# Four chunks' transposes moved from TensorE to the DMA crossbar, with the stores moved to ScalarE's queue

## The chip, the cores and the metric

One core of a Trainium2 chip. The metric is the device time of one execution in microseconds (us), median of several; runs of one kernel are compared with runs of the kernel before on the same chip in the same rounds. Besides the time, each execution gives the mean clock granted to TensorE (1.0 is full speed), and it is fast or slow (slow is over 1.5% above the fastest run of the same kernel). The experiments ran on several chips, so each is compared by its ratio to the kernel before on its own chip.

## The reference

A linear recurrence per head (retention), then a gated feed-forward layer on its output:

```python
def _attn_ref(q, k, v):                  # (4, 8, 768, 64) each
    gamma = 1.0 - 2.0 ** (-5.0 - np.arange(H))
    for t in range(S):
        state = gamma[None, :, None, None] * state + np.einsum('bhd,bhe->bhde', k[:, :, t], v[:, :, t])
        y[:, :, t] = scale * np.einsum('bhd,bhde->bhe', q[:, :, t], state)
# x = y as 3072 tokens of 512
def _moe_ref(x, w_gate, w_val, w_out):   # 512 -> 1536 -> 512
    gate = 1.0 / (1.0 + np.exp(-(x @ w_gate)))
    return gate * (x @ w_val) @ w_out
```

## The kernel before

The recurrence is computed in 24 chunks of 128 tokens. Per chunk k and q are loaded as bf16 (by GpSimd's queue, which casts), v as float32; k and q must be transposed for the scores. Chunks 0 to 11 are transposed on TensorE through PSUM (the memory that TensorE writes), with a copy back by ScalarE; chunks 12 to 23 by the DMA crossbar, that is by a DMA that transposes while it moves the data. Six blocks of 512 tokens (`t`) run the feed-forward groups, and the attention steps of the next block are put between those groups at the indices in `place`.

```python
XBAR = 12
def transposes(g):                       # chunks 4..11
    ...                                  # 8 TensorE transposes into PSUM tile tp
    nc.scalar.activation(qkT[g], tp, AX.Copy)

def xbar(g):                             # chunks 12..23
    qkT[g] = ld.tile([128, 2 * NP, C], BF16, tag="qkX", name="qkX", bufs=8)
    for i, x in enumerate((kn[g], qn[g])):
        nc.sync.dma_start_transpose(out=qkT[g][:, i * NP:(i + 1) * NP, :],
                                    in_=x.rearrange("s h d -> s (h d)"))

def down(t, sm, part):
    ...                                  # 12 matmuls into o
    ob = ffn.tile([128, D_MODEL], F32, tag="ob", name="ob")     # 3 buffers
    nc.scalar.copy(ob, o)
    nc.sync.dma_start(out=out[row:row + 128, :], in_=ob)
...
for t in range(NT):
    ...
    if t + 2 < NT:
        for g in range(4 * t + 8, 4 * t + 12):
            load_chunk(g)                # GpSimd's queue, in order
    for i, group in enumerate(groups):
        if i == len(groups) - 9:
            for g in range(4 * t + 8, 4 * t + 12):
                if XBAR <= g < NG:
                    xbar(g)
        group()
        ...                              # the attention steps whose place is i
```

Each engine takes its instructions in the program's order.

## Time and profile before

| | kernel before |
|---|---|
| time, median of the three runs at that point | 236.8 us |
| TensorE (PE) busy | 225.4 us of a span of 235.7, 1712 matmul records |
| ScalarE (ACT) busy | 91.0 us |
| DMA | full to about 124 us, then nearly idle |

The main lines of its page stand in the prediction below. First, what SyncE's own queue (SPq) waited for (who, for whom, us in total, times, longest), where the stores are L299:

```profile
SPq L299 <- ACT ob L297: 163.5, 22, 42.5
SPq L164 <- DMA kn<-in_k_dram: 15.4, 4, 9.4
```

The stores wait for the copies that fill their buffer, and SyncE can afford to wait. Second, ScalarE in time (start, duration, operation, in brackets the idle time before it and what ended it) in block 0:

```profile
47.89 0.59 ACT L297 COPY ob<-ff 128x512 f32<-128x512 f32 x1 [0.27 <-PE ff L292]
48.84 1.02 ACT L148 ACTIVATE qkT<-tp 128x1024 bf16<-128x1024 bf16 x1 [0.37 <-PE tp L146]
```

An output tile is copied, then, 0.4 us later, chunk 6's transposes are copied. On ScalarE there is no store between the two.

### The profile page before, as it was taken

How to read it: one execution, taken by the hardware profiler on the slowest of the kernel's cores; microseconds unless marked ns; L12 is line 12 of the kernel's file. 1: busy time of each engine (PE TensorE's matmuls, PEld its weight loads, DVE VectorE, ACT ScalarE, POOL GpSimd, SP SyncE). 2: the span in 40 equal slices, each digit the busy share in tenths (PEclk: the TensorE clock that was granted, in tenths of full speed). 3: DMA queues.
4: the chain of work that ended last, by engine and by line, in shares of the span. 5: the costliest groups of instructions: out<-in, count | busy, mean ns of one | idle time of the engine just before them, and what ended most of it. 6: DMA issues, size and time to landing. Idle time of an engine off the chain costs nothing.

```text
span 235.7 us, 4320 instructions
## 1 busy us (share of the span) xinstructions
PE 225.4 (96%) x1712; PEld 117.8 (50%) x1738; DVE 103.9 (44%) x178; ACT 91.0 (39%) x173; POOL 92.3 (39%) x111
## 2 busy tenths in 40 slices
PE   6779999999999999999999999999999999999994
PEld 5655644555555554444554444544444554444444
DVE  3465436375656741346641346641346641234301
ACT  8765334345455521334323333233333331333211
POOL 8999865687887367964111001111000000000000
PEclk9999999999999999999999999999999999999999
DMA  7999999999999999999992342012100012100022
GB/s 132 188 187 166 196 204 207 191 241 224 225 172 135 149 151 216 241 116 118 141 161 91 90 92 45 1 47 90 44 3 0 0 47 82 52 0 3 0 89 89
DMA packets 77555, 27.27 MB, mean 116 GB/s; under 512 B 65056, under 2 KB 73120, under 8 KB 77536
## 3 DMA queue, kind: packets, MB, share of 16 engines
q0 software_dynamic: 57616, 16.78, 69.3%
q1 hardware_dynamic: 19776, 10.16, 21.2%
q8 instruction: 13, 0.21, 0.4%
q10 hardware_dynamic: 144, 0.07, 0.1%
q14 instruction: 6, 0.05, 0.1%
HBM read 28.31 MB, written 6.29 MB: 147 GB/s over the span
## 4 chain that ended last, share of the span: by engine, by line
PE 87%; DMA 6%; POOL 3%; issue 1%; ACT 1%; DVE 1%; SPq 0%; ACTq 0%; POOLq 0%
PE ff L261 50%; PE ff L292 25%; DMA wv<-in_moe_w_val_dram 3%; PE sA L179 3%; DMA vf<-in_v_dram 3%; PE y L215 2%; PE y L191 2%; PE tp L146 2%; PE z L201 2%; PE ff L312 1%; POOL vs L169 1%; PE ff L275 1%; POOL wg L81 1%; ACT ob L297 1%; ACT qkT L148 0%
## 5 line engine op out<-in xcount | busy, mean ns | idle before, releaser
L266 DVE TENSOR_TENSOR hT<-gs,ff 128x512 bf16<-128x512 f32 (+1 forms) x72 | 48.8, 677 | 76.1 <-PE ff L261 74.5
L261 PE MATMUL ff<-xT,wg 128*128 128x512 bf16 (+1 forms) x276 | 71.5, 375 | 1.3 <-DVE xT L223 0.7
L261 PE MATMUL ff<-xT,wv 128*128 128x512 bf16 (+1 forms) x282 | 71.8, 375 | 0.9 <-DMA wv<-in_moe_w_val_dram 0.5
L265 ACT ACTIVATE gs<-ff 128x512 f32<-128x512 f32 (+1 forms) x72 | 42.3, 588 | 67.5 <-PE ff L261 67.0
L292 PE MATMUL ff<-wo,hT 128*128 128x512 bf16 x268 | 62.2, 379 | 0.6 <-issue 0.2
L261 PEld LDWEIGHTS <-wv 128*128 128x128 bf16 x288 | 28.1, 98 | 33.4 <-DMA wv<-in_moe_w_val_dram 0.9
L261 PEld LDWEIGHTS <-wg 128*128 128x128 bf16 x288 | 26.6, 98 | 30.4 <-issue 1.1
L292 PEld LDWEIGHTS <-hT 128*128 128x128 bf16 x276 | 26.0, 98 | 30.3
L297 ACT COPY ob<-ff 128x512 f32<-128x512 f32 x23 | 13.5, 586 | 50.6 <-PE ff L292 45.4
L169 POOL TENSOR_TENSOR vs<-vf,tabv 128x512 bf16<-128x512 f32 x14 | 14.5, 1047 | 46.6 <-PE y L215 41.3
L223 DVE TENSOR_TENSOR xT<-y,taby 128x512 bf16<-128x512 f32 x24 | 16.4, 685 | 20.9 <-PE y L215 20.9
L62 POOL DMA_DIRECT2D vf<-in_v_dram x23 | 20.7, 902 | 10.7 <-DMA kn<-in_k_dram 4.6
L67 POOL DMA_DIRECT2D kn<-in_k_dram x23 | 20.8, 903 | 6.2 <-DMA qn<-in_q_dram 2.2
L184 DVE TENSOR_TENSOR stA<-sA,causal 128x512 bf16<-128x512 f32 x24 | 16.5, 687 | 14.5 <-PE sB L179 14.4
L68 POOL DMA_DIRECT2D qn<-in_q_dram x23 | 20.4, 886 | 6.0 <-DMA vf<-in_v_dram 2.8
L209 ACT CAST zbd<-z 64x256 bf16<-64x256 f32 x40 | 14.7, 366 | 12.5 <-PE z L201 12.2
L185 DVE TENSOR_TENSOR stB<-sB,causal 128x512 bf16<-128x512 f32 x24 | 16.3, 681 | 0.0
L148 ACT ACTIVATE qkT<-tp 128x1024 bf16<-128x1024 bf16 x8 | 8.2, 1024 | 5.0 <-PE tp L146 5.0
L215 PE MATMUL y<-stB,vs 128*64 128x128 bf16 x96 | 9.5, 221 | 0.4 <-DVE stB L185 0.4
L215 PE MATMUL y<-stA,vs 128*64 128x128 bf16 x96 | 9.6, 221 | 0.0
L304 PE MATMUL ff<-ident 128*128 128x128 bf16 x82 | 7.1, 249 | 1.6 <-POOL ident masks.py:199 1.6
L169 DVE TENSOR_TENSOR vs<-vf,tabv 128x512 bf16<-128x512 f32 x10 | 6.9, 690 | 3.8 <-DMA vf<-in_v_dram 3.7
(58 smaller groups left out, 123.7 us busy)
## 6 DMA issues: line engine op xcount, KB each, us to landing
vf<-in_v_dram POOLq DMA_DIRECT2D x23, 256.0 KB, 8.4
out_dram<-ob SPq DMA_DIRECT2D x23, 256.0 KB, 2.0
kn<-in_k_dram POOLq DMA_DIRECT2D x23, 128.0 KB, 8.6
qn<-in_q_dram POOLq DMA_DIRECT2D x23, 128.0 KB, 8.7
wg<-in_moe_w_gate_dram POOLq DMA_DIRECT2D x6, 256.0 KB, 7.1
wv<-in_moe_w_val_dram POOLq DMA_DIRECT2D x6, 256.0 KB, 7.6
wo<-in_moe_w_out_dram POOLq DMA_DIRECT2D x4, 384.0 KB, 10.3
kf<-in_k_dram SPq DMA_DIRECT2D x1, 256.0 KB, 3.4
```

The source lines that it names most:

```text
L62: eng.dma_start(out=vf[g], in_=src(v, g))
L67: nc.gpsimd.dma_start(out=kn[g], in_=src(k, g))
L68: nc.gpsimd.dma_start(out=qn[g], in_=src(q, g))
L169: eng.tensor_tensor(vs[g], vf[g], tabv[:, g % NCH, :].unsqueeze(2).to_broadcast([C, H, D]), op=ALU.mult)
L184: nc.vector.tensor_tensor(stA[g], sc[g][0], causal4, op=ALU.mult)
L185: nc.vector.tensor_tensor(stB[g], sc[g][1], causal4, op=ALU.mult)
L215: nc.tensor.matmul(y[g][i * D:(i + 1) * D, p, :], vs[g][:, 2 * p + i, :], st[:, p, :], start=(first and p == 0), stop=True, skip_group_che ...
L223: nc.vector.tensor_tensor(xT[g // 4][:, :, col:col + C], y[g], taby[:, :, c * C:(c + 1) * C], op=ALU.mult)
L261: nc.tensor.matmul(u[:, lo:hi], w[:, kk, n1 * 128:(n1 + 1) * 128], xT[t][:, kk, lo:hi], start=(kk == 0), stop=(kk == KT - 1))
L265: nc.scalar.activation(gs[:, lo:hi], ps[0][:, lo:hi], AX.Sigmoid)
L266: nc.vector.tensor_tensor(hT[t][:, n1, lo:hi], gs[:, lo:hi], ps[1][:, lo:hi], op=ALU.mult)
L292: nc.tensor.matmul(o, hT[t][:, n1, sm * 128:(sm + 1) * 128], wo[:, n1, :], start=(n1 == 0), stop=(n1 == NFF - 1))
```

## The change

Its intent: TensorE loses 32 transposes and ScalarE four copies, as the crossbar transposes chunks 8 to 11 as soon as they land. So that nothing disturbs this, the loads of chunks 12 to 15 are held until chunk 11's k transpose is there, by a one-element GpSimd copy that reads it. SyncE's queue now waits for loads early on, so the stores go to ScalarE's queue.

```diff
-    XBAR = 12
+    XBAR = 8
+    mark = const.tile([1, 1], BF16, name="mark")
-        scale_v(g, nc.vector if g < XBAR else nc.gpsimd)
+        scale_v(g, nc.vector if g < 12 else nc.gpsimd)
-        nc.sync.dma_start(out=out[row:row + 128, :], in_=ob)
+        nc.scalar.dma_start(out=out[row:row + 128, :], in_=ob)
@@ block t == 1
-            place = [p + 2 for p in place]
+            place = [4, 5, 5, 8, 8, 11, 11, 14, 18]
+        if t == 1:
+            nc.gpsimd.tensor_copy(mark, qkT[11][0:1, 0, 0:1])
         if t + 2 < NT:
             for g in range(4 * t + 8, 4 * t + 12):
                 load_chunk(g)
+                if t == 0:
+                    xbar(g)
@@ the later blocks transpose as before
-                    if XBAR <= g < NG:
-                        xbar(g)
+            if t > 0 and i == len(groups) - 9:
+                ...                      # xbar of the next four chunks
```

## The prediction

> **What bounds the kernel now.** I read the head of the page first, then the chain of work that ended last, then the groups, the DMA issues, and last the time-ordered list around the instructions that the change touches. The page of the kernel before:
>
> ```profile
> PE 225.4 (96%) x1712; PEld 117.8 (50%) x1738; DVE 103.9 (44%) x178; ACT 91.0 (39%) x173; POOL 92.3 (39%) x111
> ...
> PE   6779999999999999999999999999999999999994
> ...
> DMA  7999999999999999999992342012100012100022
> ...
> PE 87%; DMA 6%; POOL 3%; issue 1%; ACT 1%; DVE 1%; SPq 0%; ACTq 0%; POOLq 0%
> ```
>
> The reader is to see that TensorE (PE) is full from the fourth slice on (a slice is 235.7 / 40 = 5.9 us), and that 87% of the chain is PE. Only the first 23 us belong to the loads, and the change leaves them alone. So the time falls only where PE has fewer instructions or a shorter wait. The second resource is the DMA: nines until about 21 x 5.9 = 124 us, then nearly idle. Each chunk's loads run in that full stretch, though PE rarely feels them, since they were issued early enough. The change spends this second resource to relieve the first.
>
> What can be relieved is small. From the groups, sorted by cost:
>
> ```profile
> L148 ACT ACTIVATE qkT<-tp 128x1024 bf16<-128x1024 bf16 x8 | 8.2, 1024 | 5.0 <-PE tp L146 5.0
> ...
> L146 PE MATMUL tp<-ident,qn 128*128 128x128 bf16 x32 | 3.1, 219 | 0.0
> L146 PE MATMUL tp<-ident,kn 128*128 128x128 bf16 x32 | 3.1, 219 | 0.0
> ```
>
> These are chunks 4 to 11, eight transposes each. The 219 ns is a latency; they are pipelined, and the chain merges one chunk's eight into a piece of 0.45 us (four such pieces for chunks 8 to 11: 0.46, 0.45, 0.45, 0.45). The busy column (3.1 + 3.1 for eight chunks) counts the last latency too, so I take the 0.45.
>
> **What the Trainium skill says.** "VectorE: DVE Perf Modes", section The three transpose paths, gives 390 ns for a 128x128 transpose on TensorE and 1309 ns through the DMA crossbar. In this trace the TensorE one costs about 0.45 / 8 = 0.056 us in a row: seven times less than the page's isolated figure, so the saving must not be taken from the page. "DMA: Bandwidth & Descriptors", section Issuing engines are not separate DMA queues, says that issuing from several engines saves only issue time, as all run on the same 16 DMA engines; so moving stores to ScalarE frees SyncE's queue but no bandwidth. The trace agrees that sharing hurts:
>
> ```profile
> 58.00:70.00 12.00, 11.66 (x112) 6.79 (x111) 7.10 (x12) 5.83 (x10) 9.77 (x12) 1.00 1.88 205
> 70.00:82.00 12.00, 11.89 (x105) 6.39 (x106) 8.29 (x14) 6.06 (x11) 6.71 (x9) 1.00 1.74 142
> ...
> 131.70:143.00 11.30, 11.25 (x82) 5.35 (x81) 6.09 (x10) 4.13 (x8) 0.38 (x1) 1.00 0.50 108
> ```
>
> In this table by stretch the last three columns are granted clock, DMA share and GB/s. The crossbar transposes of chunks 12 to 15 were issued from 66.8 to 82 us: total rate fell from 205 to 142 GB/s. Alone (131.7 to 143 us) a transpose landed in 2.4 to 4.0 us; among loads in 8.1 to 13.2 us. The same page, section Silent corruption: two transposing streams in flight at once, asks that transposes stay on one stream; all 24 before, and all 32 after, are SyncE's, so the stores may sit on ScalarE.
>
> **The change part by part.**
>
> Removed on PE: 32 transposes, 4 x 0.45 = 1.8 us, all on the path, as PE is full there.
>
> Removed on ScalarE: 4 copies of 1.02 us, beside PE but for one place. The time-ordered list shows it (start, duration, engine, operation; in brackets the idle time before it and what ended it):
>
> ```profile
> 60.07 0.39 PE L146 MATMUL tp<-ident,qn 128*128 128x128 bf16 x4
> ...
> 60.55 1.02 ACT L148 ACTIVATE qkT<-tp 128x1024 bf16<-128x1024 bf16 x1 [0.67 <-PE tp L146]
> ...
> 61.63 0.23 PE L179 MATMUL sA<-qkT 64*128 64x128 bf16 x1 [0.28 <-ACT qkT L148]
> ```
>
> Chunk 8's scores stood behind this copy, with PE idle for 0.3 us (its weight loads 0.45). I take 0.4 us gained.
>
> Added on ScalarE: 23 store issues. The one store that ScalarE issues in the kernel before took 0.37 us, so 23 x 0.37 = 8.5 us less 4 x 1.02 = 4.1 us: 4.4 us more on an engine at 39%. It counts only where ScalarE is on PE's path, and I find one place, late in the first token block:
>
> ```profile
> 52.44 0.59 ACT L297 COPY ob<-ff 128x512 f32<-128x512 f32 x1 [2.57 <-PE ff L292]
> ...
> 52.95 1.02 ACT L148 ACTIVATE qkT<-tp 128x1024 bf16<-128x1024 bf16 x1
> ...
> 54.07 0.23 PEld L179 LDWEIGHTS <-qkT 64*128 64x128 bf16 x8 [0.42 <-ACT qkT L148]
> ```
>
> The copy of an output tile is followed at once by chunk 7's copy, for which PE waits, and from there masks and xT lead to the next block's first matmul at 56.45. The store's issue now lies between the two copies: about 0.4 plus the wait for the copy to finish, so I charge 0.5 us. Later blocks have no such copy.
>
> Added on the DMA: 8 crossbar transposes while it is full. Loads of chunk 8 were issued at 45.94 and 46.92 and took 7.2 and 7.9 us, so k lands at 53.1 and q at 54.8. SyncE has no stores now, so it issues at once; with the 8.1 to 8.7 us of the first transposes under load, chunk 8's are there at 63.5. Who needs them: scores of chunk 8 moved from place 3 to place 5. Group 3 ended near 61.2 before, less the 0.45 of transposes, plus two groups of 1.73 us (8 matmuls of 0.216): 64.2, plus the 0.5 charged above: 64.7. Margin about 1 us. Chunk 9: q landed at 58.4, say 1.5 later now because of the transposes, plus 8.5: 68.5; scores at place 8 near 70.3. Chunk 10: 61.4 + 3 + 10 = 74.4 against 76.4. Chunk 11: about 77 against 82. The margins are thin but positive; I charge 0.4 us for one that fails.
>
> The hold: chunk 12's load was issued at 58.9 and now waits for chunk 11's transpose, 72 to 76. From there GpSimd issues 24 loads (0.9 us each, 21.6 at least; before, 58.9 to 91.0 = 32 us, of which some 8 were backlog that is now gone): 24 us, so the GpSimd multiplication for chunk 12, queued behind them, starts at 96 to 100 instead of 91.0. It is needed by chunk 12's state matmuls, at 106.3 before, 104.6 after. Chunk 12's own transposes should land near 92, against 97. So the hold is hidden, with 4 to 5 us to spare. The small GpSimd copy itself is nothing.
>
> Sum: 236.8 - 1.8 - 0.4 + 0.5 + 0.4 = **235.5 us**, 0.5% less.
>
> **The rivals.** First, the crossbar is late: chunks 8 to 10 each stall PE. For it: latencies of 10 to 13 us with several in flight, and margins of 1 to 2 us; against it: with loads 12 and on held back, less is in the queues than at 66 to 82 us. Three stalls of 1 us make 238. Second, the hold comes out too long, and chunk 12's scaled values or transposes are late: a stall near 97 to 105 us, 1 to 5 us, 236 to 240; against it are the 4 us worked out above and a DMA drained when the hold ends. Third, all is hidden and the ScalarE charge too (PE has other work queued): the full 2.2 us, 234.5. Fourth, ScalarE becomes the bound by its stores: 39% busy plus 2% speaks against it.
>
> **Range and chances.** The best case is 1.8 + 0.4 plus a little, 234.2; two late transposes or a small stall from the hold give 237.4. Faster by over 2% would need 4.7 us, twice what can be removed: 0.02. Slower by over 2% needs nearly 7 us of stalls over the gain: 0.03.
>
> **What would show it.** PE's instruction count falls by 32, its busy time by about 1.8 us (225.4 to 223.6); the group of qkT copies shrinks from 8 to 4. Waits of PE on DMA (qkX) at the scores of chunks 8, 9, 10 show the first rival; PE waiting on GpSimd's vs near 100 us, or on qkX near 97, the second. Chunk 7's scores starting 0.5 us later confirm the charge for the stores. The prediction is wrong if PE's idle time between 60 and 110 us grows by more than 2 us, or if the first 23 us differ.

## The result

| | before | changed |
|---|---|---|
| time, all runs (us) | 236.72 to 237.47 | 259.07, 259.28, 260.21, 265.02, 268.34 |
| median (of four runs each, without 259.07) | 236.95 | 262.62 |
| TensorE clock | 1.0 | 0.96 in the fast runs, 0.94 to 0.947 in the slow |
| TensorE busy (us), matmul records | 225.4, 1712 | 229.8, 1679 |

Fast runs against fast runs, the ratio is 1.0949 (95% interval 1.0909 to 1.0989): **9.5% slower**, far outside the predicted range. A ratio here is the mean time of one kernel's fast runs over that of the other's of the same rounds, so it is not quite the ratio of the medians; the changed kernel's fast runs are the three up to 260.21. The profile of the changed kernel is of a slow run (265.02 us, span 263.3); the runs differ in the clock, and the reading below is checked against experiments whose profiles are fast. Its page (in the two rows of 40 digits, a digit is the busy share of TensorE, and the clock granted to it, in tenths, in one of 40 equal slices):

```profile
PE 229.8 (87%) x1679; PEld 118.4 (45%) x1706; DVE 103.8 (39%) x178; ACT 87.5 (33%) x169; POOL 92.4 (35%) x112
...
PE   6979999600999999925999999999999999999994
...
PEclk9999999965599999985999999999999999999999
```

TensorE has two holes, in slices of 6.6 us: at 46 to 66 us and at 112 to 125 us. In and after each the granted clock drops (the slices' means go down to 0.5), so 33 fewer matmul records take 4.4 us longer. (The weight loads fell by the expected 32, from 1738 to 1706; some matmul records are missing from both traces.) The waits, in the columns used above:

```profile
ACT qkT L149 <- DMA qkX<-qn: 16.8, 1, 16.8
PE sA L180 <- ACT qkT L149: 15.5, 1, 15.5
...
PE ff L262 <- ACT ob L298: 8.0, 2, 7.6
ACT ob L298 <- DMA qkX<-kn: 8.0, 1, 8.0
ACT ob L298 <- DMA qkX<-qn: 5.9, 1, 5.9
```

TensorE waits for ScalarE, and ScalarE waits for crossbar transposes. The first of these is odd: `qkT L149` is chunk 6's copy out of PSUM, which has nothing to do with a DMA. ScalarE in time, at the place shown of the kernel before:

```profile
47.65 0.59 ACT L298 COPY ob<-ff 128x512 f32<-128x512 f32 x1 [0.27 <-PE ff L293]
64.61 0.34 ACTq L300 DMA_DIRECT2D out_dram<-ob  x1
64.99 1.02 ACT L149 ACTIVATE qkT<-tp 128x1024 bf16<-128x1024 bf16 x1 [16.76 <-DMA qkX<-qn]
```

The output tile was ready at 48.24, but its store was issued only at 64.61. Chunk 8's q transpose was issued at 55.35 and took 9.2 us: it landed at 64.5. So the **store** waited for that transpose, and chunk 6's copy stood behind the store. The chain of work that ended last has it in these words (start, duration, what), and the second hole below it:

```profile
55.35 9.18 DMA qkX<-qn
64.61 0.34 ACTq L300
...
109.64 10.68 DMA qkX<-kn
120.39 0.34 ACTq L300
```

Why would a store to memory wait for a transpose of other data? The built program says so. A semaphore is a counter that one engine or DMA raises and another waits for. In this program every hardware-queue DMA (those of SyncE and ScalarE) gets one of eight completion semaphores in turn, and before it reuses one, its engine must wait for the DMA that had it before. The start of that list, read from the built program and not from a profile, in the order in which the semaphores are handed out:

```
engine   DMA                  semaphore   must first have landed
SyncE    loads k0, q0, v0     0, 1, 2
SyncE    transpose k8, q8     3, 4
SyncE    transpose k9, q9     5, 6
SyncE    transpose k10, q10   7, 0        -, load k0
ScalarE  block 0 store 1      1           load q0 (long done)
SyncE    transpose k11, q11   2, 3        load v0, transpose k8
ScalarE  block 0 store 2      4           transpose q8
SyncE    transpose k12, q12   5, 6        transposes k9, q9
ScalarE  block 0 store 3      7           transpose k10
...
ScalarE  block 1 store 1      5           transpose k15
ScalarE  block 1 store 2      6           transpose q15
ScalarE  block 1 store 3      1           transpose k17
```

"DMA: Bandwidth & Descriptors" of the Trainium skill, section Why a DMA increments its semaphore by 16 and not by 1, gives a reason that fits such waits: two DMAs in flight on one semaphore can fool a waiter, so it asks for one per slot in flight. No run here shows a fooled waiter. Its section Anatomy of one DMA, which describes the path of GpSimd's DMAs, says where a wait is served: "any semaphore wait happens on the issuing sequencer before dispatch". The trace agrees with this for ScalarE's stores: store 2 was issued 0.1 us after q8 had landed, and block 1's third store was issued at 120.39, when k17 (issued at 109.64, 10.7 us) had just landed; that is the second hole.

The loss of this slow, profiled run adds up. Against the repaired kernel of the experiments (span 233.9, PE busy 223.8, as many matmul records): 15.5 us of waiting for chunk 6's copy, 8.0 for the output copies, and 229.8 - 223.8 = 6.0 us of slower clock make 29.5; the spans differ by 263.3 - 233.9 = 29.4 us. The fast runs (spans of 257.4 to 258.5) lose 23.5 to 24.6 us; how that splits no profile shows.

### The profile page after: what moved, and what is told of

Its sections match the earlier page's. It is cut to its first block, busy times and chain, and to the rows that moved or that the text cites. A ratio compares the mean times of both kernels' runs of the same rounds, so it can differ in the third digit from the quotient of the medians.

```text
span 263.3 us, 4259 instructions
## 1 busy us (share of the span) xinstructions
PE 229.8 (87%) x1679; PEld 118.4 (45%) x1706; DVE 103.8 (39%) x178; ACT 87.5 (33%) x169; POOL 92.4 (35%) x112
## 4 chain that ended last, share of the span: by engine, by line
PE 68%; DMA 19%; POOL 8%; issue 2%; ACT 1%; DVE 1%; SPq 0%; ACTq 0%; POOLq 0%
PE ff L262 39%; PE ff L293 20%; DMA wo<-in_moe_w_out_dram 4%; DMA qkX<-kn 4%; DMA wg<-in_moe_w_gate_dram 4%; DMA qkX<-qn 3%; DMA kn<-in_k_dram 3%; PE sA L180 2%; PE y L216 2%; POOL wg L81 1%; POOL wv L81 1%; POOL qn L68 1%; PE z L202 1%; PE y L192 1%; POOL vf L62 1%
## 5 line engine op out<-in xcount | busy, mean ns | idle before, releaser
L262 PE MATMUL ff<-xT,wg 128*128 128x512 bf16 (+1 forms) x276 | 72.7, 380 | 9.0 <-ACT ob L298 7.6
L262 PE MATMUL ff<-xT,wv 128*128 128x512 bf16 (+1 forms) x283 | 72.8, 378 | 0.8 <-ACT ob L298 0.5
L293 PE MATMUL ff<-wo,hT 128*128 128x512 bf16 x266 | 64.0, 387 | 0.7 <-issue 0.2
L180 PE MATMUL sA<-qkT 64*128 64x128 bf16 x32 | 3.4, 229 | 15.6 <-ACT qkT L149 15.5
L149 ACT ACTIVATE qkT<-tp 128x1024 bf16<-128x1024 bf16 x4 | 4.1, 1025 | 19.9 <-DMA qkX<-qn 16.8
L180 PEld LDWEIGHTS <-qkT 64*128 64x128 bf16 x64 | 2.0, 98 | 17.7 <-ACT qkT L149 16.6
## 6 DMA issues: line engine op xcount, KB each, us to landing
wo<-in_moe_w_out_dram POOLq DMA_DIRECT2D x4, 384.0 KB, 10.7
```

Source lines behind the costliest of these rows:

```text
L262: nc.tensor.matmul(u[:, lo:hi], w[:, kk, n1 * 128:(n1 + 1) * 128], xT[t][:, kk, lo:hi], start=(kk == 0), stop=(kk == KT - 1))
L293: nc.tensor.matmul(o, hT[t][:, n1, sm * 128:(sm + 1) * 128], wo[:, n1, :], start=(n1 == 0), stop=(n1 == NFF - 1))
```

## The experiments

**Theory** (rotation): stores on ScalarE wait for transposes that had their semaphore before them, and hold up ScalarE. **Rivals**: the crossbar or the hold is too slow in a full DMA; three output buffers are too few; or ScalarE's stores beside transposes are slow in themselves.

### 1. The stores back on SyncE

```diff
-        nc.scalar.dma_start(out=out[row:row + 128, :], in_=ob)
+        nc.sync.dma_start(out=out[row:row + 128, :], in_=ob)
```

> The change with one part undone: the stores go back to SyncE's queue. Theory (semaphore rotation: each hardware-queue DMA must wait until the DMA eight places earlier in the program's order has landed, and a store on ScalarE holds up ScalarE's copies while it waits): the wait of 16.8 us of chunk 6's copy vanishes, but the four stores of block 0 now stand on SyncE behind chunk 11's transposes, which wait for loads until about 70 us; with three output buffers the fourth output copy at about 56 us waits for the first store, to about 72 to 75 us, and ScalarE stalls there: 245 to 255 us. Rival (the crossbar itself is too slow or the hold too long, with stores irrelevant): stalls stay at the scores of chunks 8 and 12, about 258 us.

Measured: 253.75 us (ratio 1.0709, 1.0656 to 1.0762). Its waits:

```profile
ACT ob L298 <- DMA out_dram<-ob: 18.2, 1, 18.2
PE ff L262 <- ACT ob L298: 15.8, 1, 15.8
```

As the theory said: the wait of chunk 6's copy is gone, and the other one is there, the fourth output copy (run at 74.17 us) waiting for the first store, now behind the transposes on SyncE. So with the stores on SyncE three buffers are too few, which is a loss of its own.

### 2. The stores on SyncE and eight output buffers

```diff
+        nc.sync.dma_start(out=out[row:row + 128, :], in_=ob)
-    ob = ffn.tile([128, D_MODEL], F32, tag="ob", name="ob")
+    ob = ffn.tile([128, D_MODEL], F32, tag="ob", name="ob", bufs=8)
```

> Stores back on SyncE's queue and eight output buffers instead of three, so that nobody waits for a late store. Rotation theory: nearly all of the loss is gone, 234.5 to 236.5 us, as the prediction reckoned without its ScalarE charge; no wait of ScalarE on a DMA longer than 1 us. Rival (crossbar or hold): PE still waits for qkX or vs, over 245 us.

Measured: 235.51 us (ratio 0.9936, 0.9906 to 0.9966). That is 0.6% less than the kernel before. The whole loss is gone, with the crossbar, the hold and the places untouched. The page:

```profile
PE 223.8 (96%) x1679; PEld 116.4 (50%) x1706; DVE 104.3 (45%) x178; ACT 87.2 (37%) x169; POOL 92.2 (39%) x112
...
PE   6879999999999999999999999999999999999994
```

No hole is left, and PE's busy time is down from 225.4 to 223.8.

### 3. Eight buffers alone, and the stores on ScalarE with eight

The kernel before, and the changed kernel, each with `bufs=8` for `ob` and no other edit.

> The kernel before with eight output buffers and nothing else: the control for the runs with eight. Its stores hardly ever made ScalarE wait, so 236.5 to 237.3 us, no different from before. If it is faster by 1 us or more, the gain of the eight-buffer run is not the transposes'.

Measured: 236.49 us (0.9986, 0.997 to 1.0002): no different, so experiment 2 owes nothing to the buffers by themselves.

> The change with eight output buffers instead of three, stores on ScalarE. Its list of waits for stores is that of the change. Rotation theory: the buffers do not help, as it is the store itself that waits on ScalarE: 255 to 265 us, with the copy of chunk 6 again waiting some 16 us. Rival (the loss is that three output buffers are too few for late stores): about 236 us.

Measured: 252.99 us in its one fast run, 261.66 to 266.33 in three slow ones; no ratio could be given. Its profile (slow) has the same wait:

```profile
ACT qkT L149 <- DMA qkX<-qn: 17.0, 1, 17.0
```

Buffers do not remove the wait where the store itself blocks the engine. The rival that too few buffers explain the changed kernel's loss falls; whether they take off some of it (252.99 against 259.07 to 260.21, one run on another chip) stays open.

### 4. The kernel before with only the stores moved

```diff
-        nc.sync.dma_start(out=out[row:row + 128, :], in_=ob)
+        nc.scalar.dma_start(out=out[row:row + 128, :], in_=ob)
```

> The kernel before with only the stores moved to ScalarE's queue; no transpose added, no load held. Rotation theory, from the list of the program's waits: block 0's stores wait for nothing late, but block 1's first store shares its semaphore with chunk 16's k transpose, the second with its q, the third and fourth with chunk 17's; these land at about 94 to 103 us while the copies are ready at 86 to 95, so ScalarE stops in block 1: 243 to 252 us. Rival (the loss comes from the added transposes or the hold; my original charge for the move): 236.5 to 237.5 us.

Measured: 241.28 and 241.34 us in the fast runs, 246.01 and 250.44 in the slow (ratio of the fast 1.0178, 1.0133 to 1.0223, so by the 2% rule unclear, though clear of 1). Slower by 1.8% without a single added transpose, a little less than I expected (243 to 252 us). Its ScalarE in block 1:

```profile
85.63 0.59 ACT L297 COPY ob<-ff 128x512 f32<-128x512 f32 x1 [2.81 <-PE ff L292]
92.49 0.34 ACTq L299 DMA_DIRECT2D out_dram<-ob  x1
92.87 0.75 ACT L209 CAST zbd<-z 64x256 bf16<-64x256 f32 x2 [6.66 <-DMA qkX<-kn]
```

The copy was ready at 86.2, its store left at 92.49, and the state's copy stood behind it: block 1's first store shares its semaphore with k16, exactly as the list says. In block 0, where the list has no such pair, all four stores left at once. There, too, my original charge can be read: chunk 7's copy began 1.00 us after the output copy instead of 0.51, close to the 0.5 us charged.

### 5. One place more in the rotation

One load of 256 bytes on SyncE between chunk 9's and chunk 10's transposes of the changed kernel, which does nothing but take a semaphore:

```diff
                 if t == 0:
                     xbar(g)
+                    if g == 9:
+                        nc.sync.dma_start(out=junk, in_=v[0, 0, 0:1, :])
```

> The change with one tiny extra load of 256 bytes on SyncE's queue between chunk 9's and chunk 10's transposes; it does nothing but take one place in the rotation of the eight semaphores. By the list of the program's waits block 0's second store now waits for chunk 9's k transpose instead of chunk 8's q. Rotation theory: the long wait of chunk 6's copy on ScalarE ends when chunk 9's k has landed, at about 66 to 68 us, instead of 64.5 (chunk 8's q): 2 to 3 us longer. Rival (a fixed hardware order or a full DMA): it ends at 64.5 as before.

Measured: 258.73 us (one run, state unknown). ScalarE in time:

```profile
46.92 0.59 ACT L299 COPY ob<-ff 128x512 f32<-128x512 f32 x1 [0.27 <-PE ff L294]
68.30 0.34 ACTq L301 DMA_DIRECT2D out_dram<-ob  x1
68.69 1.02 ACT L150 ACTIVATE qkT<-tp 128x1024 bf16<-128x1024 bf16 x1 [21.17 <-DMA qkX<-kn]
```

In this run chunk 8's q landed at 54.74 + 8.1 = 62.8 us and chunk 9's k at 56.17 + 12.1 = 68.3 us. The store left at 68.30. One unrelated tiny DMA moved the wait from one transpose to the next, 5.5 us here (I had said 2 to 3, from the landings of the first profile). The total of one run says little, but the moment at which the store left is the plainest evidence of the rotation.

### 6. The stores on ScalarE, but the rotation in step

k and q of a chunk share one tile and one transpose, so that four transposes and four stores per block could fill the eight semaphores in step:

```diff
-        for i, x in enumerate((kn[g], qn[g])):
-            nc.sync.dma_start_transpose(out=qkT[g][:, i * NP:(i + 1) * NP, :],
-                                        in_=x.rearrange("s h d -> s (h d)"))
+        nc.sync.dma_start_transpose(out=qkT[g], in_=kq[g].rearrange("s h d -> s (h d)"))
@@ first attempt, block 1: the hold also waits for a hidden tile of the block
+                nc.gpsimd.tensor_copy(mark, hT[1][0:1, 0, 0:1])
@@ second attempt, instead of that: in xbar, before the transpose
+        if g >= 12 and g % 4 == 0:
+            nc.vector.memset(qkT[g][0:1, 0, 0:1], 0.0)
```

> The change as it is, stores on ScalarE, hold kept, but k and q of a chunk share one tile and are transposed by one DMA of 128x1024 instead of two of 128x512, and the marker copy on GpSimd also waits for the first hidden tile of block 1, which only moves chunk 12's transposes behind block 0's stores in the order in which semaphores are handed out. Same bytes, same engines, same queues. Rotation theory: no store of block 0 shares a semaphore with a transpose in flight, so the 16.8 us wait and nearly all the loss vanish: 234.5 to 238 us (block 1's last stores share with chunks 14 and 15, perhaps 1 or 2 us of wait). Rival (transposes beside loads, stores on ScalarE as such): 255 to 260 us as before.

Measured: 259.18 us median (fast run 250.27; the others and the profile slow). A miss in size: block 0's stores all left at once, but in block 1 the third and fourth stores waited 8.1 and 7.8 us for chunks 14 and 15, which the list does name and which I had put at 1 to 2 us. I had the pairs right and the landings wrong.

> The change with stores still on ScalarE and the hold kept; one transpose DMA of 128x1024 per chunk, and a one-element VectorE memset into the first target tile of each later block (12, 16, 20) just before its transposes, so that in the order in which the eight semaphores are handed out four transposes and four stores alternate. By the list of the program's waits no store now waits for a transpose that could be in flight (the one shared with chunk 11's is long done). Rotation theory: ScalarE's waits on qkX are gone in blocks 0 and 1, where the run before it still had 8.1 and 7.8 us of them in block 1 as its list says (chunks 14 and 15): 236 to 240 us, the rest being chunk 8's scores waiting about 3 us for the longer single transpose. Rival (stores on ScalarE beside transposes are slow in themselves, or the DMA is too full): 250 us or more.

Measured: 242.87, 244.61 and 245.78 us fast (ratio 1.0318, 1.026 to 1.0376). No store waits for a transpose any more; the waits left:

```profile
ACT ob L299 <- DMA out_dram<-ob: 5.9, 2, 3.9
PE z L203 <- POOL vs L171: 3.2, 1, 3.2
PE sA L181 <- DMA qkX<-kq: 2.1, 1, 2.1
```

So issuing stores on ScalarE beside transposes does not cost the 250 us or more of the rival. But the time is above my 236 to 240: the single transpose is late for chunk 8 (2.1 us), with three buffers two copies wait for earlier stores to land (3.9 us at most), and GpSimd's multiplication for chunk 12 comes 3.2 us late (below).

### 7. Without the hold

Experiment 2 without the GpSimd copy that holds the loads of chunks 12 to 15.

> Stores on SyncE, eight output buffers, and no hold of the loads of chunks 12 to 15. My prediction's step on the hold says that it is hidden and that without it the DMA is fuller while chunks 8 to 11 are transposed, so scores of chunks 9 to 11 wait for qkX, 1 to 4 us in all: 235.5 to 239 us. If the hold does nothing, 235.5 us.

Measured: 242.3 and 243.76 us fast (ratio 1.026, 1.0217 to 1.0302), two slow at 250; the profile is slow. The hold is worth some 2 to 3% (this ratio against 0.9936 in experiment 2 and 1.0059 in its repeat below, on three chips), more than I expected, and not where I expected it: in the slow profile TensorE waited 2.6 us for qkX but 10.6 us for GpSimd's multiplication for chunk 12, which began at 116.06 us instead of 101.90 with the hold. In the fast runs these waits must have been shorter, as the whole loss there is 5.4 to 6.8 us. By stretches (granted clock, DMA share and GB/s last), without the hold and then with it:

```profile
56.00:74.00 18.00, 15.15 (x130) 8.37 (x131) 9.22 (x16) 6.39 (x13) 8.37 (x10) 1.00 1.77 123
74.00:96.00 22.00, 21.84 (x155) 10.76 (x157) 9.70 (x16) 6.70 (x14) 5.27 (x6) 1.00 1.78 142
```

```profile
56.00:74.00 18.00, 17.26 (x140) 9.25 (x141) 11.16 (x19) 7.00 (x14) 1.86 (x4) 1.00 1.53 145
74.00:96.00 22.00, 21.84 (x156) 10.77 (x157) 8.32 (x13) 6.82 (x14) 17.28 (x20) 1.00 1.80 168
```

With loads and transposes mixed, less moved in the same time (123 against 145 GB/s, 142 against 168). In the first stretch that is so although GpSimd issued fewer loads with the hold; in the second it issued more (the fifth pair of numbers, 6 against 20 instructions). So the loads held back were through sooner, as the start of the multiplication behind them shows. That mixing is the cause of the lower rate is argued from these rates and not isolated.

### 8. Is there a version that beats both?

Experiment 2 again on another chip, and beside it the same with the scores of chunks 8 to 11 one group later (`place = [4, 6, 6, 9, 9, 12, 12, 15, 18]`).

> The same kernel as the run with stores on SyncE and eight output buffers, again beside the run above on one chip: 235.5 us, a ratio of 0.993 to 0.995 to the kernel before.

Measured: 236.81 to 239.93 us (ratio 1.0059, 1.0025 to 1.0092). The first result did not repeat. In the profile of this run TensorE waited for GpSimd:

```profile
PE z L202 <- POOL vs L170: 3.1, 1, 3.1
```

> Stores on SyncE, eight output buffers, the hold kept, and the scores of chunks 8 to 11 one feed-forward group later, so that the 0.5 us for which chunk 9's scores still waited for its transposes is covered. About 235.0 us, 0.3 to 0.5 us below the run with the places of the change, both below the kernel before (236.9). If the later places cost something at the end of block 1 (xT of chunk 11 late), 236 us or more.

Measured: 235.42 to 237.49 us, one slow run of 243.88 (ratio 0.9967, 0.9935 to 0.9998). The wait that the later places should cover was still there in its profile, 0.49 us for chunk 9's q.

Last, experiment 2 with the multiplications for chunks 12 to 15 on VectorE, so that they do not stand behind loads:

```diff
-        scale_v(g, nc.vector if g < 12 else nc.gpsimd)
+        scale_v(g, nc.vector if g < 16 else nc.gpsimd)
```

> Stores on SyncE, eight output buffers, the hold kept, the places of the change, and the multiplication of v for chunks 12 to 15 on VectorE instead of GpSimd. In the repeat of the run with stores on SyncE and eight buffers PE waited 3.1 us at chunk 12's state matmuls for GpSimd's multiplication, which stood behind the held loads until 105.98 us; that is my prediction's second rival. If that wait is the whole spread between the two runs of that kernel (235.5 and 238.5 us), this kernel is at 235.0 to 235.8 us in most rounds, a ratio of 0.992 to 0.996 to the kernel before, and PE waits for no vs near 104 us. If the spread is of the chip or of the DMA elsewhere, it stays between 236 and 239 us.

Measured: 236.03 to 237.46 us fast, two slow at 240.1 and 241.88 (ratio 0.9994, 0.9962 to 1.0025). The wait for vs is gone from its profile, which is of a run of 236.19, but the spread of the timed runs is not. So this wait is one part of the spread between rounds, not shown to be all of it; most timed rounds have no profile, and what the rest is stays open. One hint: the granted clock was 0.992 or 0.993 in three of the repeat's six rounds and 0.991 and 0.986 in this kernel's two slow ones, as it is in profiles with a hole of 3 us or more (below), so some wait of that size seems to come back in some rounds. Experiment 2's gain of 0.6% did not repeat, and no other version here gained more.

## Why the prediction was wrong

- **The step that failed** is "Added on ScalarE: 23 store issues ... so I charge 0.5 us". The issue itself was sized well (0.49 us at that very place in experiment 4). The term left out is what a store waits for before it is issued: 16.8, 5.9 and 8.0 us in the changed kernel, for transposes unrelated to it. I looked for the cost in time spent, and found the right kind of place (a store between an output copy and a copy for which TensorE waits), but took the wait to be for the copy alone. It was chunk 6's copy that stood, not chunk 7's, and "later blocks have no such copy" was wrong too: in block 1 the output copies themselves stood behind the stores. The sign that I had named for being wrong came true: TensorE's idle time between 60 and 110 us grew from 0.6 to 6.6 us.
- **The fourth rival was dismissed with the wrong measure.** "ScalarE becomes the bound by its stores: 39% busy plus 2% speaks against it." A waiting engine is not busy: in the changed kernel ScalarE's busy time fell from 91.0 to 87.5 us while TensorE waited 15.5 + 8.0 us for it.
- **A second term was missing: the clock.** TensorE's idle stretches of 15.5 and 7.6 us brought the granted clock to 0.5, and cost 6.0 us more in slower matmuls. "TensorE: Matmul & The Clock Gate" of the Trainium skill, section Why this matters for your kernels, warns against PE-idle gaps over about 3 us for this reason; the runs agree: in all 14 profiles every hole of 3.07 us or more in TensorE's work brought a stretch at a granted clock of 0.50 (the shortest hole, in the repeat of experiment 2, 3.4 us of it), and no hole of 2.75 us or less did (the longest such, in the first attempt of experiment 6).
- **What was right**, as experiment 2 shows: removed on PE, 1.8 us predicted, 1.6 us in the busy time; the copy's wait for chunk 8's scores gone; chunk 8 in time, and chunk 9 short by 0.5 us where 0.4 us had been charged for one failing margin; the hold's end, 72 to 76 predicted, 73.2 measured; the sum without the store term 235.0, measured 235.51 in that run. That this is so close is partly luck: the repeat's median was 238.51. Two sums in the prediction are off by 0.1 us (58.4 + 1.5 + 8.5 is 68.4, and 236.8 - 2.2 is 234.6); nothing hangs on them.
- **Partly right**: "the hold is hidden, with 4 to 5 us to spare". GpSimd's multiplication came at 101.9 us rather than 96 to 100, and in the repeat at 105.98, past the 104 at which it is needed. This margin is a weak point of the repaired kernel. What the hold gains was put too low (experiment 7).

## What to carry to other kernels

A DMA is a wait before it is a transfer: put it on an engine whose other work can stand behind that wait, and judge the move by what the engine will wait for in its order, not by its busy share. Where completion semaphores are handed out in turn from a small set, list for each DMA which one had its semaphore before; a DMA added to that rotation can shift which wait falls on which engine. And where stores must stand behind DMAs that land late, as they do on SyncE in experiment 2, give them enough buffers that their lateness holds up nobody.

## What the Trainium skill lacked or had wrong

- "DMA: Bandwidth & Descriptors", section Issuing engines are not separate DMA queues, says that issuing from several engines only saves issue time. The choice of engine also decides whose work stands behind the DMA's waits: with eight buffers in both, 252.99 us at best with the stores on ScalarE (experiment 3) and 235.5 with them on SyncE (experiment 2).
- The same page, section Why a DMA increments its semaphore by 16 and not by 1, asks for one semaphore per slot in flight. It lacks the case of a small set in rotation, where a DMA waits for an unrelated one: 16.8 us, and 21.2 us after one 256-byte load was added to the rotation.
- "VectorE: DVE Perf Modes", section The three transpose paths, gives 1309 ns for a 128x128 crossbar transpose and 390 ns on TensorE. It lacks what they cost in a row and under load. Here, in the kernel before, a crossbar transpose of 128x512 landed in 2.4 to 4.0 us alone and in 8.1 to 13.2 us beside loads; on TensorE eight 128x128 transposes in a row took 0.45 us. The sizes differ, so the page is not shown to be wrong.
- No page that I found says what crossbar transposes and casting loads move when they run side by side: 123 GB/s mixed and 145 GB/s with the loads held (experiment 7; the cause is not isolated).
